# Sinkhorn attention and SwiGLU: batch 0's queries split in two, its keys alone on 128 partitions, a quarter of its values loaded as fp32

## The chip, the cores and the metric

The kernel runs on one core of one Trainium2 chip. The metric is the device time of one execution in microseconds (us). The core's engines each run their own queue in order: TensorE (PE) for matmuls, VectorE (DVE), ScalarE (ACT), GpSimd (POOL), SyncE (SP); 16 DMA engines move the data.

## The reference

Five Sinkhorn steps make a mixing matrix for each batch and head; keys and values are mixed over blocks of 96 rows; each query block attends to its mixed block; a SwiGLU FFN follows.

```
P = sort_net                                  # (4, 8, 8, 8): batch, head, block, block
for _ in range(5):
    P = exp(P - max(P, -1))
    P = P / (sum(P, -1) + 1e-9)
    P = P / (sum(P, -2) + 1e-9)
k_sorted = einsum('bhij,bhjcd->bhicd', P, k_b)   # k_b: (4, 8, 8, 96, 64)
v_sorted = einsum('bhij,bhjcd->bhicd', P, v_b)
scores = (1/8) * matmul(q_b, k_sorted^T)         # per block: 96 x 96
attn = softmax(scores)
x = matmul(attn, v_sorted)  -> (3072, 512)
out = (silu(x @ w_gate) * (x @ w_val)) @ w_out   # 512 -> 1536 -> 512
```

All inputs and the output are float32 in DRAM; the kernel computes the matmuls in bf16.

## The kernel before, in words

Inputs are loaded with "natural" rows: a partition holds one (head, block) pair, 64 in a batch, and in it 96 rows of 64 elements. POOL issues all casting loads (fp32 in DRAM, bf16 in SBUF): batch 0's values in two halves, its queries whole, its keys in four pieces (`load_v`, `load_q`, `load_k`, lines 91 to 108, called at 134 to 139). Queries of batch 0 lie on partitions 64 to 127 of one tile and its keys on 0 to 63, so that one matmul per row and head pair transposes the queries (through an identity part of `rmix`) and mixes the keys (through the mixing part) at once: `kq_chunk`, line 227, 96 rows by two head halves, 192 matmuls for a batch.

Values are first copied on their partition into the order (d, c) by ACT and POOL (`copy_v`, line 117; tile `vch`), then mixed by `v_chunk` (line 238), 64 matmuls. The results land in PSUM and DVE ("v") or ACT ("s") cast them to SBUF (`drain`, line 209).

Sinkhorn runs on ACT (exp) and DVE (sums, reciprocals, products) on 32 partitions (lines 183 to 205). Beside it ACT copies values in iterations 2 and 3, DVE makes the 0/1 `mask` in iteration 1, and PE runs idle matmuls (`dots`, `fill`) into `idle_ps`. A small matmul on each iteration's `rowred` ties the fillers to it (line 425). `weights` (line 429) spreads the finished matrix over partitions by 16 matmuls, and `mix_of` multiplies it with the mask into `rmix`.

Attention goes in units of 4 (query block, head pair) combinations: `qk` (scores, exp on ACT), `av` (product with the mixed values and their row sums, then reciprocal and product on DVE into `st`), then a transpose on PE (`x_to`) and a copy into `xts`, which feeds the FFN. Unit u of a half takes head pair g = u and four query blocks. Batch 0's first four units and the FFN's first products (`early`, line 492) are written out by hand, lines 442 to 514.

Until line 515 PE, POOL, DVE and ACT run in program order. From there PE and POOL keep program order, and `merge` (line 547) sets it: the FFN blocks `ffn(n)` (384 tokens each, 12 gates and 12 values) are the main line, and units and chunks go in where their due time is reached by a running sum of costs (0.65 for a group of four matmuls). `ffn(0)` carries units 4 to 7 of batch 0 at 0.0 and 5.6; a unit's transposes follow at 1.9 and 3.6 plus a lag of 3.1.

POOL issues the FFN weights (`load_gv`) after a tiny copy, `landed`, that waits for batch 0's keys; so they don't compete with them. PSUM tiles rotate: tag "gen" has three banks, "a" and "b" two banks each, "x" one. DMAs on SP are the sort matrix at the start and, much later, outputs and transposes.

Of the kernel before, what the change touches and what calls it, by code (L numbers as in the profile page):

```python
# [9 lines left out]
FP32 = mybir.dt.float32  # L10
BF16 = mybir.dt.bfloat16
# [6 lines left out]
def kernel(  # L18
# [72 lines left out]
    def load_k(b, lo, hi):  # L91
        rows = highr if b else lowr
        nc.gpsimd.dma_start(out=kq_tile(b)[rows, lo:hi, :], in_=k_nat[b, :, lo:hi, :])
# [6 lines left out]
    def load_q(b, lo, hi):  # L100
        rows = lowr if b else highr
        nc.gpsimd.dma_start(out=kq_tile(b)[rows, lo:hi, :], in_=q_nat[b, :, lo:hi, :])
# [31 lines left out]
    load_v(0, 0, HC)  # L134
    load_v(0, HC, C)
    make_identity(nc, ident)
    load_q(0, 0, C)
    for lo, hi in ((0, 32), (32, 64), (64, 80), (80, 96)):
        load_k(0, lo, hi)
    copy_v(nc.gpsimd, 0, lowr, 0)  # L140
    copy_v(nc.gpsimd, 0, lowr, 3)
    copy_v(nc.gpsimd, 0, lowr, 5, 8, 40, D)
    landed = const.tile([R, 1], BF16)
    nc.gpsimd.tensor_copy(landed, kq_tiles[0][0:R, C - 1, D - 1:D])
    for m in range(0, 1024, 256):
        load_gv(m, m + 256)
    load_v(1, 0, C)
    for m in range(1024, DF, 256):
        load_gv(m, m + 256)
# [5 lines left out]
    for t in rmix.values():  # L155
        nc.vector.memset(t, 0.0)
# [13 lines left out]
    mask = const.tile([128, H], BF16)  # L170
    id4 = ident.rearrange("p (u h j) -> p h u j", u=2, h=H)
# [9 lines left out]

    p_ps = bank_tile("p_ps")[0:BH, 0:NB * NB].rearrange("p (i j) -> p i j", j=NB)
    for it in range(N_ITER):
        nc.scalar.activation(p_ps, p_sb if it == 0 else p_ps, AF.Exp)
        if it == 1:
            with nc.allow_low_precision("0/1 mask"):
                nc.vector.tensor_reduce(mask, id4, axis=AX.XY, op=ALU.add)
            nc.vector.tensor_copy(rmix[0][highr, 1].rearrange("p h i -> p (h i)"), ident[highr, highr])
        if it == 2:
            copy_v(nc.scalar, 0, lowr, 2, 8)  # L190
        if it == 3:
            copy_v(nc.scalar, 0, lowr, 3, 8)
        rowred = rowreds[it]
        nc.vector.reduce_sum(rowred[:, :, 0], p_ps, axis=AX.X)
        nc.vector.reciprocal(rowred, rowred)
        nc.vector.tensor_mul(p_ps, p_ps, rowred.to_broadcast([BH, NB, NB]))
        nc.vector.reduce_sum(colred[:, 0, :], p_ps.transpose([0, 2, 1]), axis=AX.X)
        nc.vector.reciprocal(colred, colred)
        if it < N_ITER - 1:
            nc.vector.tensor_mul(p_ps, p_ps, colred.to_broadcast([BH, NB, NB]))  # L200
    for lo in (0, NB // 2):
        part = slice(lo, lo + NB // 2)
        nc.vector.tensor_tensor(
            p_bf[:, part], p_ps[:, part].unsqueeze(2).to_broadcast([BH, NB // 2, H, NB]),
            colred.unsqueeze(1).to_broadcast([BH, NB // 2, H, NB]), op=ALU.mult)
    copy_v(nc.scalar, 0, lowr, 4, 8)
    copy_v(nc.scalar, 0, lowr, 5, 8, 0, 40)
# [30 lines left out]
    def v_chunk(b, at, n, eng, tag):  # L238
        rows = slice(0, 128) if b % 2 else lowr
        dst = vt_tile(b // 2)[:, b % 2]  # L240
        mix = rmix[b][rows, 0].rearrange("p a b -> p (a b)")
        tp = chunk_tile("tv", n // 8, tag).rearrange("p (l n) -> p l n", n=H * NB)
        for ld in range(n):
            col = (at + ld) * C
            nc.tensor.matmul(tp[:, ld, :], lhsT=vch[rows, col:col + 128], rhs=mix,  # L245
                             start=True, stop=True)
        drain(eng, dst[:, :, at:at + n], tp[0:C].transpose([0, 2, 1]))

    def v_pair_chunk(pair, at, n, eng, tag):
        dst = vt_tile(pair)[:, :, :, at:at + n]  # L250
# [8 lines left out]

    es, sts, xts = {}, {}, {}  # L260
    ecount = [0]

    def scores(b, u, tag):
        half, g = divmod(u, H2)
# [8 lines left out]
        for i4 in range(4):  # L273
            at = (g * NB + half * 4 + i4) * C
            for two in range(2):
                lo = two * D
                nc.tensor.matmul(pss[two][:, i4 * C:(i4 + 1) * C],  # L277
                                 lhsT=k_sb[lo:lo + D, k_at + at:k_at + at + 128],
                                 rhs=q_sb[lo:lo + D, q_at + at:q_at + at + C],
# [16 lines left out]
    def av(b, u, tag="a"):  # L296
        half, g = divmod(u, H2)
# [3 lines left out]
        for two in range(2):  # L301
            e = es[(b, u)][two]
            for i4 in range(4):
                nc.tensor.matmul(o[:, two, i4, :], lhsT=e[:, i4 * C:i4 * C + 128],  # L304
                                 rhs=vt[:, 2 * g + two, half * 4 + i4, :],
# [106 lines left out]
    idle_ps = bank_tile("idle_ps", "x")  # L412

    def fill(tile, n):
        for _ in range(n):
            nc.tensor.matmul(tile, lhsT=warm_sb[:, 0:128], rhs=warm_sb, start=True, stop=True)  # L416

    def dots(n):
        for _ in range(n):
            nc.tensor.matmul(idle_ps[0:32, 0:32], lhsT=warm_sb[:, 0:32], rhs=warm_sb[:, 0:32],  # L420
                             start=True, stop=True)

    dots(124)
    for it, n in ((1, 3), (2, 4), (3, 4), (4, 4)):
        nc.tensor.matmul(idle_ps[0:NB, 0:NB], lhsT=rowreds[it][:, :, 0], rhs=rowreds[it][:, :, 0],
                         start=True, stop=True)
        fill(idle_ps, n)

    def weights(half):
        w_ps = bank_tile(f"w_ps{half}")[:, 0:NB * B * H].rearrange("p (i b h) -> p i b h", b=B, h=H)  # L430
        for i in range(NB):
            nc.tensor.matmul(w_ps[half * R:(half + 1) * R, i].rearrange("p b h -> p (b h)"),
                             lhsT=p_bf[:, i].rearrange("p a b -> p (a b)"),
                             rhs=ident[0:BH, 0:BH], start=True, stop=True)
        return w_ps

    def mix_of(dst, b, w):
        lo = (b % 2) * R
        nc.vector.tensor_tensor(dst, mask[lo:lo + R].unsqueeze(2).to_broadcast([R, H, NB]),
                                w[lo:lo + R].transpose([0, 2, 1]), op=ALU.mult)  # L440

    w_lo = weights(0)
    mix_of(rmix[0][lowr, 0], 0, w_lo[:, :, 0])
    w_hi = weights(1)
    w_sb = const.tile([128, NB, 2, H], FP32)
    nc.scalar.copy(w_sb[lowr, :, 1], w_lo[lowr, :, 2])
    nc.scalar.copy(w_sb[highr], w_hi[highr].rearrange("p i (pair u) h -> p i pair u h", u=2)[:, :, :, 1])
    fill(idle_ps, 1)
# [6 lines left out]
    kq_chunk(0, 0, 8, "v", "gen")  # L455
    kq_chunk(0, 8, 16, "s", "a")
    kq_chunk(0, 24, 16, "v", "b")
    kq_chunk(0, 40, 8, "s", "gen")
    kq_chunk(0, 48, 8, "s", "gen")
    fill(idle_ps, 1)  # L460
    kq_chunk(0, 56, 16, "v", "a")
    fill(idle_ps, 1)
    kq_chunk(0, 72, 16, "s", "b")
    kq_chunk(0, 88, 8, "v", "gen")
    for b in range(1, B):
        rows = highr if b % 2 else lowr
        mix_of(rmix["p"][rows, b % 2] if b > 1 else rmix[1][rows, 0], b, w_sb[:, :, b // 2])
    fill(idle_ps, 4)
# [3 lines left out]
    idle_ps = bank_tile("idle_ps")  # L472
# [4 lines left out]
    fill(idle_ps, 1)  # L477
# [151 lines left out]
```

## Time and profile before

| | |
|---|---|
| median of 3 runs | 250.04 us (249.73 to 250.05) |
| span of the profiled execution | 248.0 us |
| between the span and the median | 2.0 us |
| PE, DVE, ACT, POOL busy | 240.1, 157.7, 110.3, 52.5 us |
| mean granted TensorE clock | 1.000 |
| first value matmul of batch 0 | 12.30 us |
| first score matmul of batch 0 | 20.24 us |
| first group of four FFN matmuls after the hand-written part | 27.24 us |
| first gate of FFN block 1 | 44.43 us |

A line of the order of time has start, duration, engine, line, operation, output and inputs, shape and count; in brackets is the idle time before it and what ended it. Neighbours on one engine with the same line are merged. In the table of stretches a row is a stretch of time, its length, then for each engine the busy time and the number of instructions. Fillers count as busy. In a DMA line stand the tile, the issuing queue, the number of issues, the size as it lands, and the median time from issue to landing.

### The profile page before, as it was taken

How to read it: one execution, taken by the hardware profiler on the slowest of the kernel's cores; microseconds unless marked ns; L12 is line 12 of the kernel's file. 1: busy time of each engine (PE TensorE's matmuls, PEld its weight loads, DVE VectorE, ACT ScalarE, POOL GpSimd, SP SyncE). 2: the span in 40 equal slices, each digit the busy share in tenths (PEclk: the TensorE clock that was granted, in tenths of full speed). 3: DMA queues.
4: the chain of work that ended last, by engine and by line, in shares of the span. 5: the costliest groups of instructions: out<-in, count | busy, mean ns of one | idle time of the engine just before them, and what ended most of it. 6: DMA issues, size and time to landing. Idle time of an engine off the chain costs nothing.

```text
span 248.0 us, 6193 instructions
## 1 busy us (share of the span) xinstructions
PE 240.1 (97%) x2636; PEld 141.3 (57%) x2636; DVE 157.7 (64%) x332; ACT 110.3 (44%) x187; POOL 52.5 (21%) x47
## 2 busy tenths in 40 slices
PE   7899999999999999999999999999999999999994
PEld 6376566666555556655555655565555555555543
DVE  6778689887555775857657646755764585446700
ACT  2977553453544444454642552354244334232311
POOL 7948459960059200000000000000000000000000
PEclk9999999999999999999999999999999999999999
DMA  5959999999999296010122121112111121100122
GB/s 101 211 95 166 215 189 228 194 226 211 221 170 192 53 210 164 3 42 3 45 54 52 57 62 34 44 42 78 32 42 45 39 57 55 42 22 24 42 81 88
DMA packets 39530, 24.38 MB, mean 98 GB/s; under 512 B 27728, under 2 KB 35664, under 8 KB 38992
## 3 DMA queue, kind: packets, MB, share of 16 engines
q0 software_dynamic: 21328, 14.16, 38.9%
q1 hardware_dynamic: 18176, 9.84, 14.1%
q8 instruction: 20, 0.33, 0.5%
q14 instruction: 6, 0.05, 0.1%
HBM read 28.32 MB, written 7.86 MB: 146 GB/s over the span
## 4 chain that ended last, share of the span: by engine, by line
PE 83%; DVE 7%; ACT 3%; issue 3%; DMA 2%; DVEq 0%; ACTq 0%; POOLq 0%
PE v_ps L373 23%; PE o_ps L390 23%; PE g_ps L355 22%; PE tkq L233 4%; PE av_ps L304 3%; PE qk L277 2%; DVE gs_sb L365 2%; DMA v<-in_v_dram 2%; DVE st L310 2%; PE tv L245 2%; PE idle_ps L416 1%; DVE h L378 1%; PE o_ps L406 1%; ACT th_sb L363 1%; PE x_ps L321 1%
## 5 line engine op out<-in xcount | busy, mean ns | idle before, releaser
L365 DVE SCALAR_TENSOR_TENSOR gs_sb<-th_sb,g_ps 128x384 bf16<-128x384 bf16 x96 | 52.8, 550 | 51.8 <-ACT th_sb L363 49.1
L373 PE MATMUL v_ps<-xt,wv_sb 128*128 128x384 bf16 x380 | 77.3, 326 | 0.7 <-DVE gs_sb L365 0.4
L355 PE MATMUL g_ps<-xt,wg_sb 128*128 128x384 bf16 x376 | 76.5, 326 | 0.0
L363 ACT ACTIVATE th_sb<-g_ps 128x384 bf16<-128x384 f32 x96 | 47.1, 490 | 56.0 <-PE g_ps L355 53.5
L390 PE MATMUL o_ps<-wo_sb,h 128*128 128x512 bf16 x276 | 64.0, 379 | 0.0
L378 DVE SCALAR_TENSOR_TENSOR h<-v_ps,gs_sb 128x384 bf16<-128x384 f32 x96 | 53.3, 556 | 6.6
L373 PEld LDWEIGHTS <-wv_sb 128*128 128x128 bf16 x380 | 35.4, 97 | 24.6 <-issue 2.3
L355 PEld LDWEIGHTS <-wg_sb 128*128 128x128 bf16 x376 | 34.6, 97 | 23.2 <-issue 0.3
L390 PEld LDWEIGHTS <-h 128*128 128x128 bf16 x276 | 26.3, 98 | 28.9
L395 ACT COPY o_sb<-o_ps 128x512 f32<-128x512 f32 x23 | 13.5, 585 | 50.8 <-PE o_ps L390 50.8
L124 POOL COPY vch<-v 64x1536 bf16<-64x1536 bf16 (+2 forms) x11 | 28.6, 2639 | 20.7 <-DMA v<-in_v_dram 20.7
L290 ACT ACTIVATE e_all<-qk 96x768 bf16<-96x768 f32 x30 | 22.6, 802 | 8.1 <-PE qk L277 8.1
L310 DVE TENSOR_TENSOR st<-av_ps,r_sb 96x512 bf16<-96x512 f32 x32 | 21.7, 679 | 0.2
L304 PEld LDWEIGHTS <-e_all 96*128 96x128 bf16 x256 | 12.2, 98 | 4.9 <-ACT e_all L290 0.8
L304 PE MATMUL av_ps<-vt,e_all 96*128 96x65 bf16 x256 | 13.5, 194 | 0.0
L211 DVE CAST vt<-tv 96x1024 bf16<-96x1024 f32 (+1 forms) x9 | 9.8, 1100 | 2.7 <-PE tv L255 1.6
L308 DVE RECIPROCAL r_sb<-av_ps 96x8 f32<-96x8 f32 x32 | 6.4, 199 | 7.6 <-PE av_ps L304 7.5
L213 ACT CAST vt<-tv 96x1024 bf16<-96x1024 f32 (+1 forms) x9 | 9.2, 1032 | 3.1 <-PE tv L255 1.8
L211 DVE CAST kqt<-tkq 128x1024 bf16<-128x1024 f32 (+1 forms) x7 | 7.5, 1068 | 2.7 <-PE tkq L233 2.6
L213 ACT CAST kqt<-tkq 128x1024 bf16<-128x1024 f32 (+1 forms) x7 | 6.0, 894 | 6.6 <-PE tkq L233 6.6
L416 PE MATMUL idle_ps<-warm_sb 128*128 128x512 bf16 x28 | 8.7, 409 | 0.0
L233 PE MATMUL tkq<-rmix,kq 128*64 128x64 bf16 x384 | 7.8, 197 | 0.6 <-issue 0.6
(74 smaller groups left out, 126.3 us busy)
## 6 DMA issues: line engine op xcount, KB each, us to landing
out_dram<-o_sb SPq DMA_DIRECT2D x23, 256.0 KB, 2.0
v<-in_v_dram POOLq DMA_DIRECT2D x3, 768.0 KB, 19.9
kq<-in_q_dram POOLq DMA_DIRECT2D x2, 768.0 KB, 13.6
wg_sb<-in_moe_w_gate_dram POOLq DMA_DIRECT2D x6, 256.0 KB, 8.5
wv_sb<-in_moe_w_val_dram POOLq DMA_DIRECT2D x6, 256.0 KB, 9.1
wo_sb<-in_moe_w_out_dram POOLq DMA_DIRECT2D x1, 1536.0 KB, 23.8
kp<-in_k_dram POOLq DMA_DIRECT2D x2, 768.0 KB, 15.1
q_scr<-in_q_dram POOLq DMA_DIRECT2D x2, 768.0 KB, 29.9
```

The costliest lines, as they stand in the source:

```text
L124: eng.tensor_copy(dst, src.transpose([0, 2, 1]))
L211: nc.vector.tensor_copy(dst, src)
L233: nc.tensor.matmul(tp[two * D:(two + 1) * D, lc, :], lhsT=kq_tiles[b][:, at + lc, :], rhs=rm[:, two], start=True, stop=True)
L290: nc.scalar.activation(e_all[:, n:n + 2, 0:4 * C], wide[0:C, :, 0:4 * C], AF.Exp, scale=scale)
L304: nc.tensor.matmul(o[:, two, i4, :], lhsT=e[:, i4 * C:i4 * C + 128], rhs=vt[:, 2 * g + two, half * 4 + i4, :], start=True, stop=True)
L310: nc.vector.tensor_tensor(st.rearrange("p i two d -> p two i d"), o[0:C, :, :, 0:D], r_sb.to_broadcast([C, 2, 4, D]), op=ALU.mult)
L355: nc.tensor.matmul(g_ps, lhsT=wg_sb[:, kc, ts(m, 128)], rhs=xt[:, kc, :], start=(kc == 0), stop=(kc == NKC - 1))
L363: nc.scalar.activation(th_sb, g_ps, AF.Tanh, scale=0.5)
L365: nc.vector.scalar_tensor_tensor(gs_sb, th_sb, 1.0, g_ps, op0=ALU.add, op1=ALU.mult)
L373: nc.tensor.matmul(v_ps, lhsT=wv_sb[:, kc, ts(m, 128)], rhs=xt[:, kc, :], start=(kc == 0), stop=(kc == NKC - 1))
L378: nc.vector.scalar_tensor_tensor(h_tiles[n][:, m, :], v_ps, 0.5, gs_tiles.pop(m), op0=ALU.mult, op1=ALU.mult)
L390: nc.tensor.matmul(o_ps, lhsT=h_w[:, m, ts(t3, 128)], rhs=wo_sb[:, m, :], start=(m == 0), stop=(m == NFC - 1))
```

## The change

Batch 0 alone is treated otherwise, and the order of its hand-written part is new.

- Its queries come in two loads: each takes the first or the second 384 rows of every head, which are four query blocks, cut into 16 runs of 24 rows; a load fills 128 partitions (8 heads x 16 runs) with 24 x 64 elements. The first is issued after the values, the second after the keys have landed.
- Queries no longer pass through `rmix`. `q0_chunk` transposes them by columns of the identity: 48 matmuls for a half. The first half is done in iteration 3 of Sinkhorn and cast by ACT in iteration 4; the second in FFN block 0 (`q0_rest`), cast by ACT and DVE.
- Its keys lie alone on 128 partitions, 48 rows each; `k0_chunk` mixes both row halves by a `rmix` of 128 x 2 x 64: 96 matmuls instead of 192 with four casts instead of eight.
- The first quarter of its values is loaded as fp32 by SP (`v0f`); POOL loads the rest in two pieces of three eighths. Values are copied in eighths: ACT takes 0, 2, 3 in iterations 1 to 3, POOL 1, 4, 5, 6, 7.
- `mask` has both halves and is made in iteration 2; one `mix_of` over 128 partitions fills batch 0's `rmix`, the other three move behind the second unit's `av`.
- Batch 0's first four units take two query blocks of two head pairs each, so that units 0 and 1 complete the first 192 columns of `xts`; the first FFN products come in halves of 192 columns.
- Fillers around the key matmuls go; the weights' loads become larger past column 512. In `ffn(0)` units are due at 2.0 and 6.6.

```diff
@@ loads
-    load_v(0, 0, HC)
-    load_v(0, HC, C)
+    QC = C // 4
+    q_runs = q.rearrange("b h (t j c) d -> b t h j (c d)", t=2, c=QC)
+    qk0 = natp.tile([128, C, D], BF16, name="qk0", tag="nat")
+    q0 = [qk0[:, HC + t * QC:HC + (t + 1) * QC, :] for t in range(2)]
+    k0 = qk0[:, 0:HC, :]
+    def load_q0(t):
+        nc.gpsimd.dma_start(out=q0[t].rearrange("p c d -> p (c d)"), in_=q_runs[0, t])
+    EC = C // 8
+    v0f = vnp.tile([R, 2 * EC, D], FP32, name="v0f", tag="vf")
+    nc.sync.dma_start(out=v0f, in_=v_nat[0, :, 0:2 * EC, :])
+    load_v(0, 2 * EC, 5 * EC)
+    load_v(0, 5 * EC, C)
+    load_q0(0)
     make_identity(nc, ident)
-    load_q(0, 0, C)
-    for lo, hi in ((0, 32), (32, 64), (64, 80), (80, 96)):
-        load_k(0, lo, hi)
-    copy_v(nc.gpsimd, 0, lowr, 0)
-    copy_v(nc.gpsimd, 0, lowr, 3)
-    copy_v(nc.gpsimd, 0, lowr, 5, 8, 40, D)
+    for a, rows in enumerate(halves):
+        nc.gpsimd.dma_start(out=k0[rows], in_=k_nat[0, :, a * HC:(a + 1) * HC, :])
+    for e in (1, 4, 5, 6, 7):
+        copy_v0(nc.gpsimd, e)
...
+    load_q0(1)
-    for m in range(0, 1024, 256):
-        load_gv(m, m + 256)
+    load_gv(0, 256)
+    load_gv(256, 512)
+    load_gv(512, 1024)
     load_v(1, 0, C)
-    for m in range(1024, DF, 256):
-        load_gv(m, m + 256)
+    load_gv(1024, DF)
@@ new chunks
+    def q0_chunk(t, at, n, tag):
+        dst = kqt_tile(0)[:, GI * C:2 * GI * C].rearrange("p (g t r c) -> p t g r c", g=H2, t=2, c=QC)[:, t]
+        sel = ident.rearrange("p (g two r) -> p two g r", g=H2, two=2)
+        tp = chunk_tile("tq0", n // 8, tag).rearrange("p (l g r) -> p l g r", l=n, g=H2)
+        for lc in range(n):
+            for two in range(2):
+                nc.tensor.matmul(tp[two * D:(two + 1) * D, lc], lhsT=q0[t][:, at + lc, :],
+                                 rhs=sel[:, two], start=True, stop=True)
+        return dst[:, :, :, at:at + n], tp.rearrange("p l g r -> p g r l")
+    def k0_chunk(at, n, eng, tag):
+        dst = kqt_tile(0)[:, 0:GI * C].rearrange("p (n a c) -> p a n c", a=2, c=HC)
+        rm = rmix[0].rearrange("p a (g two) i -> p two a g i", two=2)
+        tp = chunk_tile("tk0", n // 8, tag).rearrange("p (l a n) -> p l a n", l=n, a=2)
+        for lc in range(n):
+            for two in range(2):
+                nc.tensor.matmul(tp[two * D:(two + 1) * D, lc].rearrange("p a (g i) -> p a g i", g=H2),
+                                 lhsT=k0[:, at + lc, :], rhs=rm[:, two], start=True, stop=True)
+        drain(eng, dst[:, :, :, at:at + n], tp.rearrange("p l a n -> p a n l"))
@@ Sinkhorn
-        if it == 1:
+        if it == 2:
...
-            nc.vector.tensor_copy(rmix[0][highr, 1].rearrange("p h i -> p (h i)"), ident[highr, highr])
-        if it == 2:
-            copy_v(nc.scalar, 0, lowr, 2, 8)
-        if it == 3:
-            copy_v(nc.scalar, 0, lowr, 3, 8)
+        if 0 < it < 4:
+            copy_v0(nc.scalar, (0, 2, 3)[it - 1])
+        if it == 4:
+            for dst, src in early_q:
+                drain("s", dst, src)
...
+        if it > 0:
+            nc.tensor.matmul(idle_ps[0:NB, 0:NB], lhsT=rowred[:, :, 0], rhs=rowred[:, :, 0],
+                             start=True, stop=True)
+            fill(idle_ps, (3, 4, 4, 4)[it - 1])
+        if it == 3:
+            early_q = [q0_chunk(0, 0, 16, "b"), q0_chunk(0, 16, 8, "gen")]
@@ units
+    def blocks(b, u):
+        half, g = divmod(u, H2)
+        if b == 0 and half == 0:
+            return [(2 * (u % 2) + gg, 2 * (u // 2) + ii) for gg in range(2) for ii in range(2)]
+        return [(g, half * 4 + i4) for i4 in range(4)]
@@ the hand-written part
-    kq_chunk(0, 0, 8, "v", "gen")
...
-    kq_chunk(0, 88, 8, "v", "gen")
-    for b in range(1, B):
-        rows = highr if b % 2 else lowr
-        mix_of(rmix["p"][rows, b % 2] if b > 1 else rmix[1][rows, 0], b, w_sb[:, :, b // 2])
-    fill(idle_ps, 4)
+    k0_chunk(0, 16, "v", "a")
+    k0_chunk(16, 16, "s", "b")
+    k0_chunk(32, 8, "v", "gen")
+    k0_chunk(40, 8, "s", "gen")
+    fill(idle_ps, 2)
     qk(0, 0, "a")
     qk(0, 1, "b")
     qk(0, 2, "gen")
     fill(idle_ps, 2)
     av(0, 0, "a")
     fill(idle_ps, 2)
     av(0, 1, "b")
...
+    for b in range(1, B):
+        mix_of(b)
+    x_first(0, "s", "x")
+    qk(0, 3, "a")
+    av(0, 2, "b")
+    x_first(1, "s", "gen")
+    early(0, range(NKC), 0)
+    av(0, 3, "a")
+    early(1, range(NKC), 0)
+    x_first(2, "s", "x")
+    early(2, range(NKC), 0)
+    x_first(3, "v", "x")
+    for n in range(3):
+        early(n, range(NKC), 1)
     gate_out(0, 0, first[0])
     value_out(0, 0, first[1])
     gate_out(0, 1, first[2])
...
+    def q0_rest():
+        for at, n, eng, tag in ((0, 16, "s", "b"), (16, 8, "v", "a")):
+            drain(eng, *q0_chunk(1, at, n, tag))
-    merge(ffn(0), units(0, range(4, 8), (0.0, 5.6)))
+    merge(ffn(0), [(0.0, q0_rest)] + units(0, range(4, 8), (2.0, 6.6)))
```

Here `copy_v0` copies one eighth of the values, from `v0f` or from the bf16 tile; `x_first` transposes one of the new units and copies it into its 192 columns of two head pairs; `early(n, kcs, ih)` is the old `early` on 192 columns.

## The prediction

> **What bounds the kernel now.** I read the shares by engine first, then a table of busy time over five stretches, cut at the first value matmul (12.30), the first score matmul (20.24), the first full FFN group of four matmuls (27.24), the first gate of FFN block 1 (44.43), and 62.
>
> ```profile
> PE 240.1 (97%) x2636; PEld 141.3 (57%) x2636; DVE 157.7 (64%) x332; ACT 110.3 (44%) x187; POOL 52.5 (21%) x47
> ...
> core 0: us, PE busy (x) PEld busy (x) DVE busy (x) ACT busy (x) POOL busy (x), PEclk, DMA share, GB/s
> 0.00:12.30 12.30, 9.56 (x164) 5.59 (x165) 8.42 (x42) 7.60 (x11) 10.45 (x16) 1.00 0.81 156
> 12.30:20.24 7.94, 7.36 (x263) 5.87 (x263) 6.36 (x8) 5.58 (x9) 4.49 (x8) 1.00 0.74 115
> 20.24:27.24 7.00, 6.91 (x99) 4.17 (x99) 4.43 (x12) 4.85 (x9) 4.60 (x7) 1.00 1.33 174
> 27.24:44.43 17.19, 17.05 (x167) 10.60 (x165) 14.93 (x35) 8.19 (x16) 12.33 (x8) 1.00 1.25 212
> ```
>
> From 27.24 on PE has work without a break, so the end moves with two things: when that stretch begins, and how much PE work is put into it. PE's share before 27.24 says little, since fillers count as work. There I read the order of time, and the DMA issues of the first 16.5 us.
>
> ```profile
> 11.28 0.77 PE L432 MATMUL w_ps<-ident,p_bf 32*64 32x32 bf16 x16
> 12.30 2.04 PE L245 MATMUL tv<-rmix,vch 64*128 64x64 bf16 x64
> 14.27 2.16 PE L233 MATMUL tkq<-rmix,kq 128*64 128x64 bf16 x112
> 17.60 0.54 PE L233 MATMUL tkq<-rmix,kq 128*64 128x64 bf16 x23 [0.57 <-issue]
> 20.24 0.69 PE L277 MATMUL qk<-kqt 64*128 64x96 bf16 x24
> ...
> 12.75 2.52 DVE L211 CAST vt<-tv 96x512 bf16<-96x512 f32 x3 [0.59 <-PE tv L245]
> 18.18 1.89 DVE L211 CAST kqt<-tkq 128x1024 bf16<-128x1024 f32 x2 [0.99 <-PE tkq L233]
> 13.91 1.62 ACT L213 CAST vt<-tv 96x1024 bf16<-96x1024 f32 x2 [0.26 <-PE tv L245]
> 19.13 1.01 ACT L213 CAST kqt<-tkq 128x1024 bf16<-128x1024 f32 x1 [1.68 <-PE tkq L233]
> ...
> v<-in_v_dram POOLq DMA_DIRECT2D x2, 384.0 KB, 5.6
> kq<-in_q_dram POOLq DMA_DIRECT2D x1, 768.0 KB, 9.1
> kq<-in_k_dram POOLq DMA_DIRECT2D x2, 128.0 KB, 10.8
> ```
>
> Between 12.30 and 20.24 the casts of PSUM to SBUF set the pace, with a PE stop of 0.57 among them. The loads land in a row: values at 6.25 and 8.1, queries at 2.99 + 9.1 = 12.1, the last keys at 15.8.
>
> The profiled span is 248.0; the median of the runs is 250.04, so 2.0 us lie around the span. I add the sum to 250.04.
>
> **The change, part by part**
>
> *1. Until the first value matmul (12.30).* The mask reduction leaves iteration 1, and the copy into rmix goes: from exp to row sum took 4.09 to 4.61 there and 6.06 to 6.28 in iteration 2, so 0.30 is saved. Against it stand two new waits.
>
> ACT's first value copy moves from iteration 2 to iteration 1 and waits for SyncE's fp32 quarter; queued behind it is the exp of iteration 2. That exp would be ready at about 5.8, and copies follow each other on ACT at 1.4 (two in 2.44, one of them shorter), so the quarter must land by 4.35. SyncE issues it at 1.15, behind the sort matrix. Its 384 KB can't land before about 3.6 (an fp32 output of 256 KB takes 2.0), nor is it likely to be later than the first cast half, also 384 KB, at 6.25. I take 5.0, nearer the middle: it starts before the casts and then shares engines with them. Then the exp starts at 6.42, not 6.06, and the second half of p_bf ends at 11.92, not 11.56.
>
> PE gets 48 selection matmuls of the first-half queries ahead of the idle matmul and four fillers of iteration 4, and in its queue the weights, value and key matmuls stand behind. The load is half of the old one: 8.1 + (12.1 - 8.1) / 2 = 10.1, less some 0.3 for SyncE's earlier start: 9.8. 48 matmuls at 17.7 ns (112 in 2.16) and their tail end at 10.85; idle matmul and four fillers (0.22 apart) let go of PE at 11.75; sixteen weight matmuls take 0.75 and the wider mix product 0.26: 12.9 for the first value matmul. The Sinkhorn path gives 11.92 + 0.5 + 0.3 = 12.8. POOL's five copies (768 elements, half of 2.82) from 5.0 give 12.1, though it issues two DMAs fewer before them. I take 12.9: **+0.6**. The ends are 12.3 (queries by 9.2, POOL last: 0.0) and, if the half load takes as long as the whole did, 9.8 + 2.0, so 15.0 (+2.7).
>
> In the trace every load of before has 64 or 128 equal rows in HBM and the DMA share is 0.98 to 1.05 in most of the stretch from 4 to 13 us; none shows rows nested as 8 heads of 16 blocks, as the new query load has them.
>
> [...]
>
> *2. First value matmul to first score matmul (7.94).* 192 key-and-query matmuls become 96, their casts 3,072 elements a partition instead of 6,144. Value casts stay. From the first value matmul: DVE's 1024 cast ends at +2.37, which frees bank a; the key matmuls start at +2.57 (0.21 from a cast's end to the next matmul, as at 16.47 to 16.68), 32 of them take 0.74; DVE's 1024 cast (1.22) and 512 cast (0.67) end at +5.2, ACT's (1.01 and 0.60) at +5.4; scores at +5.5. **-2.4.** Keys are needed at 15.4 and should land near 13.5 (9.8 + the 3.7 that they took), so they have 1.9 of cover. The PE stop of 0.57 may return (-1.9) or be covered.
>
> *3. First score matmul to first full group (7.00).* Four units, now ordered so that two blocks of all heads come first, and 12 FFN matmuls of 384 columns become 24 of 192. Added to the path: three mix products (0.26 to 0.28 each), which before ran at 20.10 to 20.91 beside scores, now sit on DVE between the second and third unit, with the third reciprocal behind them: +0.8. The fourth unit's values wait on PE behind the first half-width gate, which waits for ACT's second xt copy behind an exp. The last xt copy then ends at about +7.2 instead of 6.1, with twelve half matmuls (85 ns) behind it, of which before had about five full ones: +8.0 in place of 7.0. **+1.0** (0 to +1.8: nothing, if the mixes find DVE idle; the whole chain without overlap).
>
> *4. FFN block 0 (17.19).* The other half of the queries is selected here: 48 matmuls at 17.7 ns and two changes of work, **+0.9** of PE; a 1024 cast on ACT and a 512 cast (0.68) on DVE come with it. The last transpose is now directly in front of block 1's first gate, whose fourth matmul needs its copy: before, transpose at 42.95, copy until 43.72, gate at 44.43. Now the copy stands behind a gate product on DVE: some 0.3 is left over. And DVE, 14.93 of 17.19 busy, frees gate banks late: 0.2. **+0.5.** The ends of this part: 0, if PE's holes take all of it (21 groups of 0.655, 32 scores, 32 value products and 16 transposes make 16.2 of 17.19), and +2.0, if the late banks cost as much as all the holes there are now on top.
>
> *No cost.* Weights: POOL issues them after keys land, some 2 us earlier than 16.06, behind 384 KB of second-half queries (2.0); the first gate wants them near 23. SyncE's next DMA is an output, tens of us later.
>
> Sum: 0.6 - 2.4 + 1.0 + 0.9 + 0.5 = **+0.6**: 250.6.
>
> **The rivals**
>
> *A. Queries land late.* The half load takes 4 us, PE stands still in Sinkhorn with weights and values queued behind, and the first value matmul is at 15.0: +2.7 for +0.6, so +2.7 in all, 252.7. For it: the unfamiliar nested rows. Against it: packets, not rows, may set the rate.
>
> *B. Faster: FFN block 0 hides what is moved into it.* If its 1.0 of PE holes and DVE's 2.3 of idle time take the second-half selection and the last transpose, part 4 is 0 and the sum is 0.6 - 2.4 + 1.0 = -0.8: 249.2. It decides at 1.1 of part 4's 1.4 taken. For it: in PE's window table 17.05 of 17.19 is called busy, but the groups make 16.2. Against it: the holes are of 0.1 to 0.3, each at a bank or a switch.
>
> *C. SyncE's quarter lands last.* At 6.25, Sinkhorn slips 1.6, values start near 14.0 and the sum is +1.7: 251.7. Against it: it is first on the engines.
>
> **How the numbers follow.** Chances: my sum (249.7 to 251.2) 0.44, A 0.20, B 0.26, C 0.10. 0.2% is 0.5 us, about what can be told from no change. The forecast's own range is half under 250.54. So faster is B with a little of mine, 0.28; same 0.20; slower 0.52. The range leaves out a tenth at each side: 248.9 to 252.9.
>
> **What the profile after would show.** Right: selection matmuls start near 9.8, values near 12.9, scores near 18.4, the first full group near 26.4, block 1's first gate at 45. Wrong in part 1: selection after 11 (A), or an exp after 7 (C). In part 2: key matmuls waiting for DMA. In part 3: full group under 7.5 after the scores. In part 4: block 0 shorter than 17.6. The keys' new layout failing to shorten casts, since their runs are the same 16, would undo most of it.

## The result, and the profile after

The changed kernel takes 261.42 us (median of four; 259.3 to 263.6) against 249.88 for the kernel before in the same session: a ratio of 1.043, 95% interval 1.039 to 1.047, slower by 11 us. My forecast was 250.6, at most 252.9. The profiled execution has a span of 259.6 (before 248.0). Some single executions, the longest of these four among them, took 1.5% or more longer than the fastest of their kernel; the ratios and the later medians leave them out, but the profiles of three runs below come from such executions (values cast alone; 16 rows with a selection tile; 224 idle matmuls, 355 us long and read for the order of events alone).

The shares by engine, and the table of stretches cut at the same events as before: first value matmul, first score matmul, first full FFN group, first gate of block 1.

```profile
PE 243.2 (94%) x2641; PEld 143.9 (55%) x2641; DVE 157.0 (60%) x329; ACT 110.6 (43%) x187; POOL 50.6 (20%) x44
```

```profile
core 0: us, PE busy (x) PEld busy (x) DVE busy (x) ACT busy (x) POOL busy (x), PEclk, DMA share, GB/s
0.00:17.00 17.00, 10.84 (x212) 6.42 (x213) 8.09 (x40) 8.29 (x12) 11.15 (x16) 0.80 0.75 129
17.00:22.19 5.19, 4.26 (x162) 3.71 (x161) 4.33 (x5) 4.23 (x7) 4.49 (x7) 1.00 0.34 48
22.19:32.58 10.39, 8.35 (x108) 6.31 (x109) 5.13 (x13) 4.87 (x9) 5.03 (x8) 0.78 1.31 191
32.58:55.26 22.68, 20.32 (x214) 12.46 (x212) 15.77 (x36) 9.16 (x16) 13.48 (x9) 0.88 1.21 181
```

| stretch | before | after | difference | forecast |
|---|---|---|---|---|
| to the first value matmul | 12.30 | 17.00 | +4.70 | +0.6 |
| to the first score matmul | 7.94 | 5.19 | -2.75 | -2.4 |
| to the first full FFN group | 7.00 | 10.39 | +3.39 | +1.0 |
| FFN block 0 | 17.19 | 22.68 | +5.49 | +1.4 |
| all that follows | 203.6 | 204.3 | +0.8 | 0 |

PE is no longer without a break, and its granted clock, 1.00 throughout before, is 0.78 to 0.88 in three of the four stretches. The order of time names the waits, and the DMA issues (tile, queue, number, size, us from issue to landing) the loads behind them:

```profile
7.52 1.70 ACT L156 CAST vch<-v0f 64x768 bf16<-64x768 f32 x1 [3.34 <-DMA v0f<-in_v_dram]
9.13 0.20 ACT L286 ACTIVATE p_ps<-p_ps 32x64 f32<-32x64 f32 x1
...
14.15 1.02 PE L258 MATMUL tq<-ident,qk 128*64 128x64 bf16 x48 [0.33 <-DMA qk<-in_q_dram]
17.00 2.02 PE L237 MATMUL tv<-rmix,vch 64*128 64x64 bf16 x64 [0.38 <-DVE rmix L478]
27.11 0.50 PE L532 MATMUL g_ps<-xt,wg_sb 128*128 128x192 bf16 x4 [0.72 <-DMA wg_sb<-in_moe_w_gate_dram]
48.46 1.46 PE L433 MATMUL v_ps<-xt,wv_sb 128*128 128x384 bf16 x4 [2.36 <-DMA wv_sb<-in_moe_w_val_dram]
...
18.51 0.80 POOL L109 DMA_DIRECT2D wg_sb<-in_moe_w_gate_dram  x1
25.40 0.78 POOL L109 DMA_DIRECT2D wg_sb<-in_moe_w_gate_dram  x1 [1.83 <-DMA qk<-in_q_dram]
27.35 0.75 POOL L109 DMA_DIRECT2D wv_sb<-in_moe_w_val_dram  x1 [1.18 <-DMA wg_sb<-in_moe_w_gate_dram]
```

```profile
v0f<-in_v_dram SPq DMA_DIRECT2D x1, 384.0 KB, 6.3
qk<-in_q_dram POOLq DMA_DIRECT2D x1, 384.0 KB, 11.7
qk<-in_q_dram POOLq DMA_DIRECT2D x1, 384.0 KB, 7.2
```

SyncE's quarter lands at 7.5 and holds the exp of iteration 2 until 9.13. The first-half queries land at 14.15 (2.44 + 11.7), and PE's weights and value matmuls stand behind their selection. The second half (7.2 to landing, issued at 17.89) stands ahead of the FFN weights. GpSimd is even stopped in its issuing: by the profile, the slab at 25.40 waited for that query load. The chain of waits says the same; it is DMA from 4.2 to 17.3, from 18.5 to 27.1 and from 27.4 to 48.4:

```profile
4.19 13.11 DMA qk<-in_k_dram
...
18.51 8.56 DMA wg_sb<-in_moe_w_gate_dram
...
27.35 21.06 DMA wv_sb<-in_moe_w_val_dram
48.46 1.46 PE v_ps L433 x4
```

### The profile page after: what moved, and what is told of

It reads as the page before. It is cut to its first block, busy times and chain, and to the rows that moved or that the text cites. A ratio compares the mean times of both kernels' runs of the same rounds, so it can differ in the third digit from the quotient of the medians.

```text
span 259.6 us, 6203 instructions
## 1 busy us (share of the span) xinstructions
PE 243.2 (94%) x2641; PEld 143.9 (55%) x2641; DVE 157.0 (60%) x329; ACT 110.6 (43%) x187; POOL 50.6 (20%) x44
## 4 chain that ended last, share of the span: by engine, by line
PE 71%; DMA 16%; DVE 5%; issue 3%; ACT 2%; POOL 1%; DVEq 0%; POOLq 0%; ACTq 0%
PE o_ps L450 22%; PE v_ps L433 21%; PE g_ps L415 20%; DMA wv_sb<-in_moe_w_val_dram 8%; DMA qk<-in_k_dram 5%; DMA wg_sb<-in_moe_w_gate_dram 3%; PE tkq L225 3%; PE av_ps L364 2%; DVE gs_sb L425 2%; PE qk L338 2%; DVE h L438 1%; PE o_ps L466 1%; DVE st L370 1%; ACT th_sb L423 1%; PE tv L237 1%
## 5 line engine op out<-in xcount | busy, mean ns | idle before, releaser
L433 PE MATMUL v_ps<-xt,wv_sb 128*128 128x384 bf16 x380 | 78.9, 331 | 2.9 <-DMA wv_sb<-in_moe_w_val_dram 2.4
L415 PE MATMUL g_ps<-xt,wg_sb 128*128 128x384 bf16 x376 | 77.3, 328 | 0.1
L433 PEld LDWEIGHTS <-wv_sb 128*128 128x128 bf16 x380 | 35.6, 99 | 27.1 <-issue 2.9
L455 ACT COPY o_sb<-o_ps 128x512 f32<-128x512 f32 x23 | 13.5, 586 | 50.8 <-PE o_ps L450 48.0
L122 POOL COPY vch<-v 64x1536 bf16<-64x1536 bf16 (+1 forms) x8 | 22.3, 2825 | 27.7 <-DMA v<-in_v_dram 27.7
L351 ACT ACTIVATE e_all<-qk 96x768 bf16<-96x768 f32 x31 | 23.4, 802 | 7.4 <-PE qk L338 7.4
L276 PE MATMUL idle_ps<-warm_sb 128*128 128x512 bf16 x21 | 7.4, 475 | 0.0
L158 POOL COPY vch<-v 64x768 bf16<-64x768 bf16 x4 | 5.9, 1524 | 0.0
L203 DVE COPY xt<-x_ps 128x384 bf16<-128x384 bf16 x9 | 3.2, 351 | 4.4 <-PE x_ps L381 4.4
## 6 DMA issues: line engine op xcount, KB each, us to landing
wv_sb<-in_moe_w_val_dram POOLq DMA_DIRECT2D x2, 512.0 KB, 18.5
```

Of the source, the lines that this page charges most:

```text
L122: eng.tensor_copy(dst, src.transpose([0, 2, 1]))
L203: nc.vector.tensor_copy(dst, src)
L351: nc.scalar.activation(e_all[:, n:n + 2, 0:4 * C], wide[0:C, :, 0:4 * C], AF.Exp, scale=scale)
L415: nc.tensor.matmul(g_ps, lhsT=wg_sb[:, kc, ts(m, 128)], rhs=xt[:, kc, :], start=(kc == 0), stop=(kc == NKC - 1))
L433: nc.tensor.matmul(v_ps, lhsT=wv_sb[:, kc, ts(m, 128)], rhs=xt[:, kc, :], start=(kc == 0), stop=(kc == NKC - 1))
L455: nc.scalar.copy(o_sb, o_ps)
```

## The experiments

The first theory had two causes: the query loads use half of the DMA engines (E), and SyncE's quarter is late (S). The rivals were the half clock (C) and the wide weight slabs (W).

**16 rows instead of 8.** The slowest dimension of the query loads becomes 16.

```diff
-q_runs = q.rearrange("b h (t j c) d -> b t h j (c d)", t=2, c=QC)
+q_runs = q.rearrange("b h (t j c) d -> b t j h (c d)", t=2, c=QC)
-sel = ident.rearrange("p (g two r) -> p two g r", g=H2, two=2)
+sel = ident.rearrange("p (r g two) -> p two g r", g=H2, two=2)
```

> Both loads of batch 0's queries are read as 16 blocks of 8 heads instead of 8 heads of 16 blocks, and the selection matrix is permuted to match; all else is the changed kernel. Theory E (the two query loads run on half of the DMA engines because their slowest dimension is 8): first-half queries land at 10 to 11 instead of 14.15, the keys near 15 instead of 17.4, the weights are issued near 16.5 instead of 18.5; the exp of iteration 2 stays at 9.1, since SyncE's quarter is still there, so the first value matmul comes at 15.0 to 15.6 instead of 17.0; the wait for the last value weights at 48 mostly goes. Time 255.5 (253.5 to 257.0). Theory S (SyncE's fp32 quarter takes the engines first and delays all that comes behind): queries still land after 13, first value matmul at 16.5 or later, time 259 to 261.5. Theory C (the halved clock is the cost, and loads matter only through it): between the two, with half clock gone from 28 to 35 but the landings unchanged.

Measured: 262.4, ratio 1.048 (1.044 to 1.052): no gain, and my number was 7 off. The loads moved the way E said, the first by less: the first-half queries landed at 12.71, 10.3 after issue (E had them at 10 to 11, the changed kernel at 14.15), weights were issued at 16.69 (E: 16.5), and no group waited for a weight. The first value matmul came at 18.55, later than the changed kernel's 17.00 and not at E's 15.0 to 15.6. Two new costs ate the gain:

```profile
13.76 2.97 PE L258 MATMUL tq<-ident,qk 128*64 128x64 bf16 x48
...
20.96 1.36 PE L268 MATMUL tk<-rmix,qk 128*64 128x64 bf16 x75 [0.38 <-DVE vt L203]
25.06 0.75 PE L268 MATMUL tk<-rmix,qk 128*64 128x64 bf16 x21 [2.74 <-issue]
```

The selection takes 2.97 instead of 1.02, with its identity columns now read eight elements apart (0.95 from a contiguous tile in the runs below); the second half costs the same 2.97 again in FFN block 0. And PE stops for 2.74 in the middle of the key matmuls with no wait that the profile shows. So the edit tested two things at once; the next runs take them apart.

**The fp32 quarter undone.** The values come by two casting loads of 384 KB, as before; ScalarE copies eighths 0 and 2 in iterations 2 and 3, and 3 after Sinkhorn.

```diff
-nc.sync.dma_start(out=v0f, in_=v_nat[0, :, 0:2 * EC, :])
-load_v(0, 2 * EC, 5 * EC)
-load_v(0, 5 * EC, C)
+load_v(0, 0, HC)
+load_v(0, HC, C)
```

> The fp32 quarter of the values is undone: two casting loads of 384 KB on POOL's queue as before the change, ScalarE copies two eighths in iterations 2 and 3 and one after Sinkhorn; the query loads are those of the changed kernel. Theory E: the exp of iteration 2 is back at 6.1 to 6.4, but the queries land at 13 to 14 all the same, PE stands still for them, first value matmul at 16 or later, weights 0.5 to 1.5 earlier: 258.5 (257 to 260). Theory S: queries land at 10, first value matmul at 13.4 or earlier, time 252 (250.5 to 253.5).

Measured: 257.3, ratio 1.028 (1.022 to 1.033), in E's range. The exps are on time (5.84, 7.91), yet the queries land at 13.6 and PE waits 3.87 for them, so the first value matmul is at 18.03. S alone is not the cause.

```profile
13.66 1.49 PE L256 MATMUL tq<-ident,qk 128*64 128x64 bf16 x48 [3.87 <-DMA qk<-in_q_dram]
```

**Both edits.**

> Both edits at once: query loads read as 16 blocks of 8 heads, and values by two casting loads. This leaves the selection of queries inside Sinkhorn, the keys on 128 partitions, the new order of units and the wide weight slabs, so it tests the rest of my sum (+0.6 on 250.04, with no wait for SyncE). Theory E plus S as two separate causes: queries near 10, first value matmul at 13 to 13.5, first score 5.2 to 5.5 later, first full group 8 later, no DMA wait at 48: 251.0 (249.8 to 252.5). If one of the two causes is everything, the time equals that of the run that removes that one. If the half clock or the weight slabs are causes of their own, it stays above 253.

Measured: 259.4, ratio 1.034 (1.028 to 1.039): a miss, for the reasons of the first run. Queries land at 11.5 and the two halves of the keys at 12.9 and 14.3; then the selection takes 2.97 and PE stops for 1.85 at the same key matmul.

**Weight slabs of 256 columns throughout**, as before the change.

```diff
-load_gv(512, 1024)
+load_gv(512, 768)
+load_gv(768, 1024)
 load_v(1, 0, C)
-load_gv(1024, DF)
+load_gv(1024, 1280)
+load_gv(1280, DF)
```

> The weights are loaded in slabs of 256 columns throughout, as before the change, instead of 256, 256, 512, 512; all else is the changed kernel. Theory W (the 512-column slab is why value group 8 of FFN block 0 waits at 48: its 128 columns come only with the whole 512 KB): the 256 KB slab that group 8 needs lands about 2.5 earlier, the wait of 2.36 goes, and so does the half clock behind it (1.3): 257.7 (256.5 to 259.0). Theory E (everything on the queue is late because of the loads ahead): the tail of the queue is as late as before, the wait moves to the next slab, two groups on: 260.5 (259.5 to 261.8).

Measured: 258.7, ratio 1.033 (1.029 to 1.038), inside W's range. The first line is value group 8, the second group 10: the slab lands 3.2 earlier than the wide one (48.46), but group 8 still waits, since PE comes to it earlier too (its first full group is at 30.48, there 32.58), and group 10 waits again. So W had the gain right and E had right that the tail of the queue stays late:

```profile
45.28 0.82 PE L435 MATMUL v_ps<-xt,wv_sb 128*128 128x384 bf16 x4 [2.06 <-DMA wv_sb<-in_moe_w_val_dram]
49.28 0.82 PE L435 MATMUL v_ps<-xt,wv_sb 128*128 128x384 bf16 x4 [0.58 <-DMA wv_sb<-in_moe_w_val_dram]
```

The profiled execution has a recorded clock of 1.00 and took 257.84 (its four idle matmuls at 10.12 took 1.89, as at half clock in the changed kernel, so the record can lack an early stretch); two others at 0.98 took 259.02 and 259.64. So the 1.2 to 1.8 between them can't be put down to the half clock by these figures.

**16 rows, and the permuted selection matrix in a tile of its own**, so that matmuls read it in contiguous pieces.

```diff
+sel = const.tile([128, 2, H2, 16], BF16)
+nc.gpsimd.tensor_copy(sel, ident.rearrange("p (r g two) -> p two g r", g=H2, two=2))
```

> The run with the query loads read as 16 blocks of 8 heads once more, but the permuted selection matrix is first copied into a tile of its own, so that matmuls read it in contiguous pieces. Theory P (that run was slow because of the strided selection matrix, 62 ns a matmul where 21 was usual, and because weights issued earlier held up the load of PE's code, 2.74 of stop with no visible wait): selection takes 1.0 instead of 2.97 both times, the first value matmul comes at 15.3 to 16.0, the stop between key matmuls is under 0.7, the waits for weights stay away: 256.0 (253.5 to 258.0). Theory R (reading by 16 rows is no gain at all, the end is set elsewhere): 260 to 262.

Measured: 256.9, ratio 1.023 (1.015 to 1.031), in P's range, though two of its points failed: the stop between key matmuls stayed (2.27, P had it under 0.7), and the first value matmul came at 17.23 instead of 15.3 to 16.0.

```profile
13.81 1.49 PE L260 MATMUL tq<-sel,qk 128*64 128x64 bf16 x48
...
23.27 0.75 PE L270 MATMUL tk<-rmix,qk 128*64 128x64 bf16 x21 [2.27 <-issue]
```

Selection is 1.49 in a stretch at half clock, and 0.95 at full clock in the next run. The DMA view shows, between 20.8 and 22.0, a packet of a queue that the profile names `instruction`:

```profile
q8 instruction: 1, 0.02, 5.1%
```

By its record this packet has 16 KB and starts at 20.86, and there is none between 17.2 and then. The weights were issued from 15.82 on. PE goes on 1.42 after the packet ends.

**The same, with the casting loads of values.** SyncE's quarter is gone; selection in Sinkhorn, keys on 128 partitions, the order of units and wide slabs stay.

> The same with the two casting loads of values in place of SyncE's fp32 quarter. What is left of the change: selection inside Sinkhorn, keys on 128 partitions, the order of units, wide weight slabs. Theory P: queries land at 11.5, selection 1.0, weights and first value matmul at 14.0 to 14.6, first score 5.2 later, first full group 8 later, no DMA wait in FFN block 0: 252.2 (250.5 to 254.5). Theory R: over 257. If PE's code load again falls behind the weights, a stop of 2 or more between key matmuls and 254 to 256.

Measured: 252.8 (ten executions, 251.9 to 253.9), ratio 1.009 (1.006 to 1.012); expected 252.2. Selection is at 10.73, weights at 12.70; the value matmuls then wait for GpSimd's five copies. The prediction had these ending at 12.1; here they end at 14.89 (15.13 in the changed kernel, where queries were later still), and the expectation of this run left them out:

```profile
14.95 2.32 PE L238 MATMUL tv<-rmix,vch 64*128 64x64 bf16 x64 [1.82 <-POOL vch L159]
```

```profile
0.00:14.95 14.95, 9.32 (x210) 6.13 (x212) 8.11 (x40) 8.52 (x13) 11.42 (x18) 1.00 0.70 133
14.95:20.88 5.93, 5.44 (x163) 5.03 (x164) 4.43 (x5) 3.78 (x5) 5.87 (x10) 0.71 0.86 118
20.88:28.88 8.00, 6.43 (x109) 4.74 (x110) 4.62 (x12) 4.85 (x9) 3.42 (x5) 1.00 1.35 202
28.88:46.61 17.73, 17.73 (x214) 11.27 (x213) 15.85 (x36) 9.19 (x17) 11.04 (x4) 1.00 1.11 213
```

No stop and no wait for weights, though the clock was 0.71 between values and scores. The block of 17.73 is my part 4 without disturbance: +0.54 on 17.19.

**The same, with slabs of 256 columns.**

> The same again with weight slabs of 256 columns throughout. Theory P: with the queue early enough no group waits for a slab, so the slab width does nothing: within 0.7 of the run before this one. Theory W (wide slabs cost by themselves): 1 to 2.5 below it.

Measured: 254.2, ratio 1.013 (1.009 to 1.018): neither theory; 1.5 above the run before it. FFN block 0 is 17.73 here as well and waits for no slab. The difference lies ahead of it: values start at 15.34, and from there to the scores it takes 7.04 at a clock of 0.52, there 5.93 at 0.71. Why the clock fell lower was not separated.

**Idle matmuls in the place of the wait for weights** (13 ahead of value group 8 in the changed kernel).

```diff
+if (n, m) == (0, 8):
+    for _ in range(13):
+        nc.tensor.matmul(v_ps, lhsT=warm_sb[:, 0:128], rhs=warm_sb[:, 0:TW], start=True, stop=True)
```

> The changed kernel with 13 idle matmuls of 384 columns on PE just ahead of value group 8 of FFN block 0, in the place where PE waits 2.36 for its weights. Theory C (the stop of PE brings the half clock of 48.5 to 52, which costs 1.3 to 1.7): granted clock 1.00 there, 259.8 (258.8 to 260.6). Theory N (half clock comes from the earlier stops and is not set off by this one): 261.4, or up to 0.5 more if the idle matmuls outlast the wait.

Measured: 259.1, ratio 1.034 (1.029 to 1.039), in C's range. The stretch that had half clock in the changed kernel has it no more, and holds 33 matmuls instead of 19. Changed kernel first, then this run:

```profile
48.50:52.00 3.50, 3.50 (x19) 1.90 (x20) 0.80 (x2) 0.49 (x1) 3.50 (x2) 0.52 1.08 196
```

```profile
48.50:52.00 3.50, 3.50 (x33) 2.25 (x32) 2.98 (x7) 0.98 (x2) 3.50 (x2) 1.00 1.15 178
```

The 2.3 have two parts. Group 8 starts 0.72 earlier (47.74 instead of 48.46), because its slab lands earlier; the half clock from 28.0 to 34.8, which this execution did not have either, doesn't move it, since group 8 waits for the slab. From there to block 1's first gate the same 44 matmuls take 1.63 less, inside C's 1.3 to 1.7. That is the price of the half clock behind this wait. Changed kernel first:

```profile
48.46:55.26 6.80, 6.80 (x44) 4.03 (x45) 3.76 (x9) 1.47 (x3) 6.80 (x7) 0.75 1.17 163
```

```profile
47.74:52.91 5.17, 5.17 (x44) 3.33 (x45) 3.70 (x9) 1.47 (x3) 5.17 (x4) 1.00 1.16 174
```

**100 idle matmuls more at the start** of the 16-row run with selection tile (`dots(224)`).

> The run with 16 rows and a selection tile (fp32 quarter kept), with 224 instead of 124 of the small idle matmuls at the start. They run while PE waits for Sinkhorn anyway, and they move every later matmul 100 places on in PE's code, so that the block of code whose lack is supposed to stop the key matmuls is asked for some 100 matmuls earlier, ahead of the weights. Theory L (the stop of 2.27 between key matmuls is PE's code, loaded behind the weights): the stop goes under 0.5 at that place, first score to first full group unchanged, 254.6 (253.0 to 256.0). Theory M (the stop is something else, a bank or a cast): it stays at the same key matmul and the time at 256 to 258.

Measured: 257.1, ratio 1.030 (1.026 to 1.033): no gain. The stop left the key matmuls (96 without one) and came up among the idle matmuls instead, from 7.26 to 11.18, behind a 16 KB packet that ran from 8.21 to 9.81 beside values and queries. That fits a stop that belongs to a place in PE's code, as L has it (moved by 100 matmuls, it came up elsewhere), but shows no mechanism. But the time is M's (256 to 258; L had 253 to 256), and the order of events is that of one profile.

**Copies balanced** on the 252.8 run: GpSimd four copies, ScalarE four, one query cast on VectorE, three mix products on GpSimd, the fourth unit's values ahead of the first gate.

```diff
-for e in (1, 4, 5, 6, 7):
+for e in (1, 5, 6, 7):
     copy_v0(nc.gpsimd, e)
@@ it == 4
-for dst, src in early_q:
-    drain("s", dst, src)
+copy_v0(nc.scalar, 3)
+copy_v0(nc.scalar, 4)
```

> The best run so far (16 rows, selection tile, casting loads of values; 252.77) with the rest of its path shortened: GpSimd makes four of the eight value copies instead of five, ScalarE the fourth between its last exp and the query casts, one query cast goes to VectorE behind the Sinkhorn products; the three mix products of the other batches go from VectorE to GpSimd, and the fourth unit's values are multiplied ahead of the first half-width gate. Theory: first value matmul at 13.5 (there 14.95), first score 5.5 later, first full group 7.6 later, block 0 17.7: 44.3 for block 1's first gate, 250.7 (249.8 to 252.0). Rival (the half clock that follows PE's stops takes the gain): 252 to 253.5.

Measured: 251.8, ratio 1.007 (1.005 to 1.009); expected 250.7, inside the range. First value matmul at 14.23 (still 0.97 of wait for GpSimd's copies), then 5.87, 7.88 and 17.74. This is the fastest form found, and it does not beat the kernel before.

**Two thirds of the second selection between the first scores**, in place of four idle matmuls; two idle ones stay ahead of the scores.

```diff
 qk(0, 1, "b")
+drain("v", *q0_chunk(1, 0, 8, "gen"))
 qk(0, 2, "gen")
-fill(idle_ps, 2)
+drain("v", *q0_chunk(1, 8, 8, "x"))
 av(0, 0, "a")
-fill(idle_ps, 2)
 av(0, 1, "b")
```

> The run before with two thirds of the second-half selection taken out of FFN block 0 and put between the first scores, in place of six idle matmuls of 512 columns, its casts on VectorE, which waits there for 2.1. Theory F (the 0.95 of PE in block 0 is paid in full, since nothing hides PE work there): block 0 shortens by 0.6, 250.1 (249.0 to 251.2), which would be level with the kernel before. Theory G (VectorE's casts delay the first reciprocals and the clock drops without the idle matmuls): 251 to 253.

(The expectation counts six idle matmuls; four were taken out.) Measured: 253.1, ratio 1.011 (1.008 to 1.013): just above theory G's time (251 to 253), with one cause more than G had.

```profile
22.02 0.34 PE L383 MATMUL x_ps<-ident,st 96*128 96x96 bf16 x4 [0.87 <-DVE st L372]
24.98 0.80 PE L534 MATMUL g_ps<-xt,wg_sb 128*128 128x192 bf16 x4 [0.92 <-issue]
```

VectorE's casts delay the first transpose, another packet of 16 KB ends at 23.65, and PE resumes at 24.98. From 24.1 to 31 the clock is 0.5, and the stretch from score to full group takes 11.01.

**Weights issued behind the mix product**, on the 16-row run with selection tile (quarter kept).

```diff
+nc.gpsimd.tensor_copy(landed, rmix[0][:, 1, H - 1, NB - 1:NB])   # after rmix[0] is made
 load_gv(0, 256)
```

> The run with 16 rows and a selection tile (fp32 quarter kept; stop of 2.27 between key matmuls), with one more tiny copy on GpSimd, which reads the batch-0 mix matrix and stands ahead of the weights' issue: the weights are issued when PE has just gone into its value matmuls, near 17.6 instead of 15.8. Nothing else is moved. Theory L (PE's code block for the last key matmuls is asked for when the value matmuls begin, and then waits behind the weights on the DMA engines): the packet of 16 KB comes before 19 instead of at 20.9, the stop between key matmuls is under 0.5, first value to first score 5.2 to 5.6 instead of about 7.5, although the weights come 1.8 later; 254.8 (253.2 to 256.5). Theory M (the stop has another cause): it stays at 2 and over, the weights' waits come back, 257 to 260.

Measured: 255.2, ratio 1.022 (1.020 to 1.024). The time is in L's range, but it can't be told from the run without the hold, that is, without the tiny copy that keeps the weights back (1.023, 1.015 to 1.031), so no gain by the hold is shown. The packet starts at 19.55 instead of 20.86 (L: before 19), the stop is 1.03 instead of 2.27 (L: under 0.5), and from first value to first score it takes 5.98 (L: 5.2 to 5.6): L's direction, half of its size. I put the rest down to the second half of the queries, which is still ahead of the packet; no run shows it. Although the weights come 1.95 later, nothing waits for them:

```profile
22.02 0.51 PE L272 MATMUL tk<-rmix,qk 128*64 128x64 bf16 x21 [1.03 <-issue]
```

```profile
qk<-in_q_dram POOLq DMA_DIRECT2D x1, 384.0 KB, 4.7
```

```profile
23.21:31.22 8.01, 6.44 (x109) 4.75 (x109) 4.61 (x12) 4.84 (x9) 3.24 (x5) 1.00 1.31 204
31.22:48.95 17.73, 17.73 (x215) 11.28 (x214) 15.85 (x36) 9.19 (x17) 11.78 (x6) 1.00 1.09 206
```

The same 384 KB of second-half queries take 4.7 to landing, not 7.2. The last value slab is issued at 23.52 and lands at 42.6, in the changed kernel at 27.35 and 48.4.

These two traces show theory E itself. In both there is a stretch of 2.4 us in which, of the kernel's data, almost only the second-half queries are in flight. With 8 as slowest dimension (changed kernel, first line) the DMA share is 0.47 of 16 engines, so some 7.5 packets in flight on average, and 58 GB/s move; with 16 (this run) it is 1.02, some 16 packets, and 151 GB/s:

```profile
19.00:21.40 2.40, 2.02 (x99) 1.76 (x98) 2.21 (x4) 1.97 (x3) 2.40 (x4) 1.00 0.47 58
```

```profile
16.60:19.00 2.40, 2.02 (x77) 2.01 (x72) 1.63 (x3) 1.32 (x4) 1.42 (x3) 1.00 1.02 151
```

## Why the prediction was wrong

As ratios of about 250 us, the runs split the loss like this: from 1.043 to 1.022 when the query loads are read by 16 rows (with a selection tile, and weights behind the mix product); from 1.022 to 1.009 when SyncE's quarter goes as well (that run also issues the weights without the hold and has no stop; the hold itself made no difference that could be told); 0.009 left. That is some 5.2, 3.4 and 2.2 us.

1. *Queries at 9.8.* The failed step. I halved the row of a load that read 64 whole rows, and took it for a load of 8 heads by 16 runs. The row could not show what that costs, since no load of before had such rows. The runs do: half of the DMA share (0.47 against 1.02) and so half of the packets in flight (some 7.5 against 16), and 7.2 against 4.7 to landing for the same bytes. The first half landed at 14.1 instead of 9.8. (The Sinkhorn path beside it, 11.92 + 0.5 + 0.3, makes 12.7 and not 12.8; nothing rests on it.) Rival A had the load late, at 4 us for the half, but priced only the first value matmul. It left out that keys (landed seen at 17.43, not 13.5) and weights stand behind the same load.
2. *SyncE's quarter at 5.0, at the latest 6.25.* It landed at 7.5. I took it to be first and finished first, while it shares the engines with the casting loads (from 2.4 to 7.6 its queue takes 43% of the 16 engines' time and theirs 64%); its end by the first cast half was no bound at all. The exp of iteration 2 began at 9.13, not 6.42: rival C's mechanism, at 3.1 later than the kernel before (6.06) where C had 1.6. In the same part GpSimd's copies were mis-sized: they ended at 15.13 and not at 12.1, and in the run at 252.8 they alone held the values for 1.82.
3. *"No cost" for the weights.* The largest miss. I had them issued near 14 behind 2.0 of second-half queries. They were issued at 18.51, behind a load of 7.2, and the wider slabs, which I did not price, made value group 8 wait for a whole 512 KB: +3.39 and +5.49 instead of +1.0 and +1.4. With 16 rows, a selection tile and held weights both stretches return to 8.01 and 17.73.
4. *Part 2, -2.4.* Right: -2.75. Its premise on the keys was wrong (13.5), but since everything ahead was late too, no key matmul waited.
5. *Part 3, +1.0.* Right as a price of its own: 8.0 in three runs without a wait for weights.
6. *Part 4, +1.4.* Mis-sized: +0.54 undisturbed. FFN block 0 hides 0.9 of the 1.4: rival B's direction, short of the 1.1 at which B would have decided. What the direct sequence of last transpose and next gate costs is inside that 0.54.
7. *The clock.* No step had it. After several of PE's stops the matmuls ran at half rate (19 matmuls in the 3.5 us from 48.50 at a clock of 0.52, 33 at 1.00 in the run with 13 idle ones), so a stop was partly paid twice: 1.63 behind the wait of value group 8. How much of the 11 us the other half-clock stretches cost, the runs don't separate, since the executions that kept the clock also had earlier loads.
8. *The PE stop of 0.57*, which the prediction put among the casts. In the kernel before it stands behind a 16 KB packet from 15.20 to 16.07, as the stops of the last section do; that it "may return" came true there with up to 2.74.

The direction was right mostly by luck: slower had 0.52, by +0.6 from terms that were not what made the kernel slower. Even with all three loads put right, the change loses 1.7 to 2.3 us, at the first value matmul above all (14.23 to 14.95 instead of 12.30), which takes back what the shorter key stage gives.

## What to carry to other kernels

Price a reshaped load by its own slowest dimension and not by the bytes of an old one (here the same 384 KB took 7.2 us with 8 and 4.7 with 16), and then move every load behind it on the queue by the same delay, to the last slab of weights. Before an edit is called free, look for what it puts ahead of others: data ahead of weights (value group 8 waited 2.36), weights ahead of a packet of the instruction queue (a stop of 2.27, and of 1.03 with the weights later), a wait ahead of an exp (9.13 instead of 6.06). If a repair brings nothing, look in its trace for what it newly costs before giving up its theory.

## What the hardware showed that I had not expected

**PE's stops behind 16 KB packets.** Seven times in the first 60 us PE stopped for 0.5 us or more with no wait shown, and went on 1.3 to 1.6 us after a packet of 16 KB on the instruction queue had ended:

| run | packet, start to end | PE goes on | stop |
|---|---|---|---|
| kernel before | 15.20 to 16.07 | 17.60 | 0.57 |
| 16 rows | 22.74 to 23.70 | 25.06 | 2.74 |
| both edits | 21.06 to 21.95 | 23.40 | 1.85 |
| 16 rows, tile | 20.86 to 21.85 | 23.27 | 2.27 |
| weights behind mix | 19.55 to 20.45 | 22.02 | 1.03 |
| second selection early | 22.70 to 23.65 | 24.98 | 0.92 |
| 224 idle matmuls | 8.21 to 9.81 | 11.18 | 3.92 |

Most packets of 16 KB are followed by no stop: of seven in the first 60 us of the kernel before, one was followed by such a stop, and of five in the changed kernel none. There one ran from 17.86 to 18.80, as the weights' issue began (18.51), with a DMA share of 0.03 from 17.0 to 18.7, and PE did not stop; that the late queries hid this cost is a guess. That these packets are PE's code is inferred from the queue's name, place and time; no run shows it directly.

**Half clock after half-idle stretches.** In the changed kernel the granted clock was 0.50 from 7.52 to 14.35, from 28.00 to 34.83 and from 48.48 to 51.89; the distances between these times are 6.83, 13.65, 6.83, 13.65 and 3.41. In the 3.41 us ahead of each fall PE was busy 1.48 (4.11 to 7.52), 1.95 (24.59 to 28.00) and 1.05 (45.07 to 48.48). The clock also fell after 2.05 (second selection early, 20.72 to 24.13), 1.58 (the 252.8 run, 13.1 to 16.5) and 2.79 (both edits, 15.81 to 19.22). It stayed at 1.00 after 2.47 (13 idle matmuls, 25.22 to 28.63), 1.77 (256-column slabs with 16 rows, 5.06 to 8.47) and 2.00 (weights behind mix, 18.81 to 22.22). So between 1.77 and 2.79 both happened, and no sharp limit is shown.

**A strided moving operand.** 48 selection matmuls of 64 columns took 2.97 with identity columns eight bf16 elements apart (16 rows, at 36.79) and 0.95 from a contiguous tile (the 252.8 run, at 10.73), both at full clock.
